# Attention and feed-forward on one core: key rows placed by DMA, first shift rows written by two engines, another order of the prologue and another schedule table

## The chip, the core and the metric

The kernel runs on one core of a Trainium2 chip. A core has a matrix engine (TensorE, PE in the profile, whose weight loads are listed as PEld), VectorE (DVE), ScalarE (ACT), GpSimd (POOL) and SyncE (SP, which here issues nearly all DMAs). Each engine runs its own instruction list in order; semaphores tie them together. The metric is the device time of one execution in microseconds; less is better.

## The reference

For a sequence of 2048 rows of width 512, the kernel mixes multi-query attention (32 heads of 16, one shared key and value head) with a feed-forward block, by a gate for each row:

```python
q = (x @ wq)                      # 32 heads of 16
k = x @ wk                        # one head, 16 wide
v = x @ wv
p = softmax(q @ k.T * 16 ** -0.5)
a = (p @ v) @ wo
b = silu(x @ w1) @ w2             # 512 -> 1792 -> 512
g = sigmoid((x * gate_w).sum(-1))
out = g * a + (1 - g) * b         # all in float32
```

## The kernel before

**Pairs of float16.** Each float32 operand of a product is split into a float16 upper part and a float16 rest; a product is the sum of three float16 matmuls (`product3`). For the scores the three terms are put into the contraction rows instead: per head group the moving tile `qb_[...]` holds, from partition 0 or 64 on, 16 rows of the queries' upper part, the same 16 again, 16 rows of their rest, and then two shift rows; `KT` holds against them the keys' upper part, their rest, their upper part, and two rows of the constant `ONE`. One matmul over 50 rows so gives the score less a shift that keeps the exponential in range.

**The prologue** (`first_pass`) loads x, transposes it on PE (`T00` to `T33`: chunk and tile), splits it on ScalarE and VectorE (`te`, `tl`), forms keys and values (`K0..`, `K1..`, four steps each over the contraction) and the first two blocks of queries (`Q0`, `Q1`). The order of all engines' work is written out by hand in the string `ORDER`; the name of each step stands for a function in the table `do`, and `BANK` gives the PSUM bank of each. Each engine's instructions run in the order in which these names appear. Before the change the steps behind the keys are:

- `k1`, `k2`: the keys' upper part (ScalarE) and rest (VectorE); `vr`: values and gate sums copied out of PSUM (ScalarE); `mx`, `mxa`, `prep`, `kab`: a bound on the keys by way of a maximum, a matmul and a mask;
- `pl0` to `pl3` (`k_places`): matmuls with 0/1 matrices `selA`, `selB` that put the keys of one chunk of 512 into their rows, and `KT0` to `KT3`, which copy them out of PSUM and add the constant rows (`m_one`); three on ScalarE, `KT3` on VectorE;
- `qs`, `ql`, `qa`: a query block's upper part, rest and absolute value; `qd` writes it to DRAM, and `lq` (`load_q`) reads it back into the rows of `qb_`, six DMAs for the first round;
- `bnd`, `s1`, `qbs`: the bound for each query (matmul with `kab`), its scaling to a shift row on ScalarE, and `shift_rows`, two DMAs that copy the first shifts into row 48 of each half of `qb_[0]`, with two more that store the shifts to DRAM (`q_shift`);
- `V`, `VO`, `sig`: transposed values and gate sums copied out by VectorE, and the gate's exponential on ScalarE; `lo`: range checks on VectorE; `st`, `sl`: first weight pieces; `d4`, `d2`: dummy matmuls.

**The attention loop** (`attention`) has 32 rounds (4 chunks of queries, 4 blocks, 2 halves) of 16 steps over the keys, and each step has two score groups: eight concurrent matmuls (line 1418) and one exponential over 128x1024 on ScalarE (line 1424), 1024 in all. Between score groups PE does the sums over the probabilities (line 1522), the feed-forward and projection products (line 1072), VectorE forms the low parts `L` of the probabilities (line 1443), and weight pieces come in one after another through two buffers `raw` (line 306 loads, 323 and 324 split). The order of all this is made when the program is built, by a small planner in the kernel: it keeps an estimated clock for each engine (`pe`, `act`, `dve`, `pool`) and chooses what PE and VectorE do next by twelve parameters (`Way`), which the table `WAYS` gives anew for every eight score groups. `SENT` is the planner's count of PE instructions sent at the loop's start and `BEHIND` VectorE's starting clock.

**The end.** The last four products are evicted by VectorE (line 1033) into `acc`, and SP sends each to the output (line 1036). Then every engine reads a flag and branches (lines 1671, 1672) past a second pass, which runs only if a range was left; SP passes the semaphores of the outstanding DMAs there. DMAs take eight semaphores in rotation.

Of the kernel before, what the change touches and what calls it, by code (L numbers as in the profile page):

```python
# [12 lines left out]
AF = mybir.ActivationFunctionType  # L13
OP = mybir.AluOpType
# [17 lines left out]
SENT, BEHIND = 162, 0.5  # L32
# [132 lines left out]
def kernel(  # L165
# [53 lines left out]
    kab = consts.tile([128, 32], F16)  # L219
# [142 lines left out]
    def masks(cst):  # L362
# [4 lines left out]
        hj = cst.tile([128, 32], F32)  # L367
        nc.gpsimd.iota(hj, pattern=[[16, 32]], base=0, channel_multiplier=0, allow_small_or_imprecise_dtypes=True)
# [11 lines left out]
        selA = cst.tile([128, 8, 16], F16)  # L380
        selB = cst.tile([128, 8, 16], F16)
        nc.gpsimd.memset(selA, 0.0)
        nc.gpsimd.memset(selB, 0.0)
        for b in (0, 2, 4, 6):
            nc.gpsimd.tensor_copy(selA[:, b], sel_k[:, b])
        for b in (1, 5):
            nc.gpsimd.tensor_copy(selB[:, b], sel_k[:, b])
# [14 lines left out]
    def load_q(q, c, o, rb, shifts):  # L402
# [3 lines left out]
        for f in range(2):  # L406
            b, queue = 64 * f, nc.sync
            queue.dma_start(q[b:b + 16], v[f, rb][:, :, 0])
            queue.dma_start(q[b + 16:b + 32], v[f, rb][:, :, 0])
            queue.dma_start(q[b + 32:b + 48], v[f, rb][:, :, 1])  # L410
            if shifts:
                queue.dma_start(q[b + 48:b + 48 + shifts], u[f, rb][0:shifts])
# [115 lines left out]
    def q_bound(pu, qa):  # L528

        for h in range(2):  # L530
            nc.tensor.matmul(pu[32 * h:32 * h + 32], kab[64 * h:64 * h + 64], qa[64 * h:64 * h + 64], start=True, stop=True)  # L531
# [6 lines left out]
    def first_pass():  # L538
        with ExitStack() as pro:
# [27 lines left out]
            rows = lambda c: slice(64 * (c % 2), 64 * (c % 2) + 16)  # L567
# [7 lines left out]
            BANK = {"T00": 7, "T01": 2, "T02": 4, "T03": 3, "T10": 7, "T11": 2, "Q0": 4, "T13": 3, "T20": 7, "T21": 2,  # L575
            "T23": 3, "T22": 5, "T12": 1, "T31": 7, "T30": 2, "T33": 3, "T32": 5, "K0": 1, "K1": 7, "Q1": 2, "pl1": 3,
            "pl0": 5, "prep": 4, "bnd": 1, "pl3": 3, "pl2": 7, "V0": 4, "V1": 5}
            BY_VECTOR = (3,)
            ORDER = """
            T00 T01 te00 te01 T02 tl00 T03 d4 tl01 te02 wkva tl02 te03 wkvd Wa0 tl03 Wd0 T10 T11 te10 Q00 te11 tl10  # L580
# [1120 lines left out]
```

## Time and profile before

| what | us |
|---|---|
| median of three runs (lowest, highest) | 1020.99 (1018.49, 1023.15) |
| the profiled execution | 1018.2 |
| its span, first to last instruction | 1016.3 |
| start of the span to the first exponential | 30.87 |
| first exponential to the end of the last | 968.7 |
| from there to the end of the span | 16.7 |
| ScalarE busy / PE busy / VectorE busy in the span | 988.3 / 1005.0 / 861.2 |

The times of the rows count from the first instruction of the span. A row of the timeline is: start, length, engine, line, operation, what it writes and reads with shapes, count of merged instructions, and in brackets how long the engine was idle before and what ended that. A row of a group ends in busy time, mean ns of one, and idle time before it. SPq is SP's queue issuing a DMA; the row doesn't show when it lands. The rows on which the argument rests are shown in the prediction.

### The profile page before, as it was taken

What the parts mean: (1) busy time and instruction counts of PE and PEld (TensorE: products, weight loads), DVE (VectorE), ACT (ScalarE), POOL (GpSimd) and SP (SyncE); (2) the same over time, 40 slices, a digit from 0 to 9 for tenths busy, and PEclk for the clock granted to TensorE, in tenths of its full rate; (3) what the DMA queues carried; (4) which work ended last, traced back from release to release, by engine and by line L of the source; (5) the groups of instructions that cost most, each with busy time, mean ns of one, the idle gap of its engine ahead of it and who ended that gap; (6) DMA issues with size and microseconds to landing.
All of it is one profiled execution on the core that took longest, in us unless ns stands there. A gap on an engine that the chain in (4) does not pass through costs nothing.

```text
span 1016.3 us, 67134 instructions
## 1 busy us (share of the span) xinstructions
PE 1005.0 (99%) x31724; PEld 586.7 (58%) x31724; DVE 861.2 (85%) x809; ACT 988.3 (97%) x1117; POOL 417.2 (41%) x278
## 2 busy tenths in 40 slices
PE   9999999999999999999999999999999999999997
PEld 5556656565555566656566566565556555555553
DVE  7888888898999998888888878888878878888886
ACT  6999999999999999999999999999999999999993
POOL 2053044362372245456345253835234264344620
PEclk9999999999999999999999999999999999999999
DMA  7212112000001100000001100000000100000001
GB/s 267 66 54 85 56 55 74 23 12 24 12 4 44 33 23 12 23 8 19 13 12 33 44 21 6 22 13 12 23 12 15 44 22 28 13 12 7 10 5 44
DMA packets 23314, 33.14 MB, mean 33 GB/s; under 512 B 5497, under 2 KB 14074, under 8 KB 23034
## 3 DMA queue, kind: packets, MB, share of 16 engines
q1 hardware_dynamic: 22602, 28.74, 8.8%
q8 instruction: 249, 4.08, 1.6%
q14 instruction: 31, 0.25, 0.1%
q10 hardware_dynamic: 432, 0.07, 0.0%
HBM read 20.26 MB, written 8.52 MB: 28 GB/s over the span
## 4 chain that ended last, share of the span: by engine, by line
PE 79%; ACT 15%; DVE 2%; issue 2%; DMA 1%; SPq 0%; DVEq 0%; ACTq 0%
PE pm L1072 30%; PE pv L1522 27%; PE S L1418 20%; ACT P L1424 14%; DVE L L1443 1%; ACT e L1086 1%; DMA xn<-in_A_x_dram 1%; PE b L595 1%; PE b L615 1%; PE pm L531 0%; DVE acc L1033 0%; PE b L247 0%; DVE mxs L257 0%; PE b L248 0%; PE b L249 0%
## 5 line engine op out<-in xcount | busy, mean ns | idle before, releaser
L1424 ACT ACTIVATE P<-S 128x1024 f32<-128x1024 f32 x1024 | 953.5, 1124 | 0.9 <-PE S L1418 0.5
L1443 DVE TENSOR_TENSOR L<-P 128x2048 f16<-128x2048 f32 x234 | 560.4, 2409 | 33.6 <-ACT P L1424 31.5
L1418 PE MATMUL S<-qb,KT 50*32 50x512 f16 x8192 | 439.8, 380 | 1.2 <-ACT P L1424 0.3
L1418 PEld LDWEIGHTS <-KT 50*32 50x32 f16 x8192 | 201.5, 89 | 240.5 <-issue 148.6
L1522 PE MATMUL pv<-P,VF 64*32 64x256 f32 (+1 forms) x6208 | 321.3, 468 | 0.0
L1072 PE MATMUL pm<-w2s,H 64*32 64x512 f16 x5184 | 264.9, 375 | 0.6 <-issue 0.5
L1072 PE MATMUL pm<-xs,w1s 64*32 64x512 f16 x5376 | 254.6, 375 | 0.0
L1093 POOL CAST H<-e 128x512 f16<-128x512 f32 x56 | 81.0, 1447 | 247.6 <-DVE e L1091 247.6
L1344 POOL TENSOR_TENSOR U<-T,U 128x512 f32<-128x512 f32 x31 | 83.2, 2682 | 229.0 <-DVE U L1339 229.0
L1522 PEld LDWEIGHTS pv<-P,VF 64*32 64x32 f32 x6208 | 126.7, 106 | 32.5 <-issue 3.2
L1072 PEld LDWEIGHTS <-H 64*32 64x32 f16 x5184 | 117.8, 92 | 37.4 <-issue 1.6
L1072 PEld LDWEIGHTS <-w1s 64*32 64x32 f16 x5376 | 110.6, 92 | 42.9 <-issue 1.8
L1094 POOL TENSOR_TENSOR H<-e,H 128x512 f16<-128x512 f32 x56 | 107.6, 1922 | 4.5
L1522 PE MATMUL pv<-P,VP 64*32 64x512 bf16 x1872 | 103.6, 387 | 0.0
L1072 PE MATMUL pm<-xs,wqs 64*32 64x512 f16 x1344 | 100.7, 375 | 0.0
L1522 PE MATMUL pv<-L,VP 64*32 64x512 f16 x1872 | 100.4, 374 | 0.0
L1522 PEld LDWEIGHTS <-VP 64*32 64x32 f16 x3744 | 65.4, 92 | 29.0 <-issue 6.7
L1091 DVE SCALAR_TENSOR_TENSOR e<-e,pm 128x512 f32<-128x512 f32 x56 | 38.4, 686 | 41.5 <-ACT e L1086 41.0
L1072 PE MATMUL pm<-wo_s,O 64*32 64x512 f16 x1440 | 66.5, 375 | 0.0
L1372 POOL CAST O<-T 128x512 f16<-128x512 f32 x15 | 23.3, 1556 | 73.5 <-DVE T L1370 73.5
L1345 POOL TENSOR_TENSOR C<-U 128x240 f32<-128x240 f32 x31 | 51.3, 1656 | 2.4
L1033 DVE SCALAR_TENSOR_TENSOR acc<-pm,g,acc 128x512 f32<-128x512 f32 x46 | 34.2, 746 | 19.3 <-PE pm L1072 19.2
(174 smaller groups left out, 535.6 us busy)
## 6 DMA issues: line engine op xcount, KB each, us to landing
qb<-qd SPq DMA_DIRECT2D x192, 32.0 KB
raw<-in_B_w_dram SPq DMA_DIRECT2D x22, 256.0 KB
xn<-in_A_x_dram SPq DMA_DIRECT2D x8, 512.0 KB
out_dram<-acc SPq DMA_DIRECT2D x16, 256.0 KB
qd<-qx SPq DMA_DIRECT2D x14, 256.0 KB
w1r<-in_B_w_dram SPq DMA_DIRECT2D x2, 512.0 KB
raw<-in_A_wo_dram SPq DMA_DIRECT2D x4, 256.0 KB
qb<-sh SPq DMA_DIRECT2D x62, 2.0 KB
```

The source lines that it names most:

```text
L1033: nc.vector.scalar_tensor_tensor(a, po, gate[:, n:n + 1], a, op0=OP.mult, op1=OP.add)
L1072: nc.tensor.matmul(self.bank[32 * m:32 * m + 32], l(i, rows, 32 * m), r(j, rows), start=first, stop=last)
L1091: nc.vector.scalar_tensor_tensor(e, e, 1.0, ph, op0=OP.add, op1=OP.mult)
L1093: nc.gpsimd.tensor_copy(H[:, 0], e)
L1094: nc.gpsimd.tensor_tensor(H[:, 1], e, H[:, 0], op=OP.subtract)
L1344: eng.tensor_tensor(U, T, U, op=OP.add)
L1345: eng.tensor_tensor(C[:, :, 1:16], z[:, :, 1:16], z[:, :, 17:32], op=OP.add)
L1372: eng.tensor_copy(O[:, 0], OT)
L1418: nc.tensor.matmul(sc[32 * m:32 * m + 32, f], KT[b:b + 50, k0:k0 + 32], qtile[i][b:b + 50, j], start=True, stop=True)
L1424: nc.scalar.activation(P[:, 2 * j:2 * j + 2], sc, AF.Exp, scale=scale_of(c, o))
L1443: nc.vector.tensor_tensor(L[s], P, upper(P), op=OP.subtract)
L1522: nc.tensor.matmul(pvs[i][h][32 * j:32 * j + 32, cols], a[r], b[r, j, cols], start=start, stop=rest == n)
```

## The change

The layout of the contraction rows changes: the two shift rows now stand at 32 and 33 of each half (and the constant rows of `KT` with them), and the third group of 16 at 34 to 49.

- The keys are put into `KT` by DMA from `k1` and `k2` (`ka`, `kb`: 24 DMAs on SP in all) and no more by `pl` and `KT`; the constant rows are written at the start by four VectorE instructions. `selA` and `selB` aren't made in the first pass.
- The first shifts are computed by four small matmuls (`bq0`, `bq1`), whose result stands in partitions 32 and 96, and written straight into `qb_[0]` by ScalarE (`sq0`) and VectorE (`sq1`), two instructions each over one partition. `bnd` and `s1` remain for the stored shifts (`qsh`).
- The second query block is stored by two DMAs instead of one.
- `BANK` and `ORDER` are written anew; `WAYS` has another 128 entries; `SENT` is 158 for 162, `BEHIND` 1.0 for 0.5.
- At the very end a memset of one column of the output tile `accs[13]`, the second of the last four, and a one-column matmul on it are added. The count of DMAs ahead of the last output changes, and with it the semaphore that it takes.
- The second pass (not run here) follows the new layout.

```diff
-SENT, BEHIND = 162, 0.5
+SENT, BEHIND = 158, 1.0
 WAYS = [
...
-            queue.dma_start(q[b + 32:b + 48], v[f, rb][:, :, 1])
+            queue.dma_start(q[b + 34:b + 50], v[f, rb][:, :, 1])
             if shifts:
-                queue.dma_start(q[b + 48:b + 48 + shifts], u[f, rb][0:shifts])
+                queue.dma_start(q[b + 32:b + 32 + shifts], u[f, rb][0:shifts])
...
+            for c in range(NCH):
+                nc.vector.tensor_scalar(KT[:, c * 512:c * 512 + 512], still, m_one, None, op0=OP.add)
             constants()
...
             ORDER = """
-            T00 T01 te00 te01 T02 tl00 T03 d4 tl01 te02 wkva tl02 te03 wkvd Wa0 tl03 Wd0 T10 T11 te10 Q00 te11 tl10
-            T13 tl11 Q01 te13 T20 tl13 T21 te20 T23 te21 tl20 T22 te23 T12 tl21 te22 T31 tl23 te12 T30 tl22 te31 Q02
-            te30 tl12 T33 tl31 T32 te33 tl30 K000 te32 tl33 Q03 st0 tl32 st1 K010 sl0 Wa1 qs0 K100 st3 ql0 K020 qa0
-            sl3 qd0 K110 st2 sl1 K030 sl2 K120 k10 Wd1 lq vr0 K130 k20 mx0 Q10 k11 pl1 vr1 mx1 Q11 KT1 mxa pl0 k21
-            prep Q12 KT0 kab bnd lo Q13 s1 pl3 qs1 qbs pl2 KT3 V0 qa1 ql1 V1 d2 KT2 VO0 VO1 qd1 sig
+            T00 T01 te00 te01 T03 tl00 wkva T02 d4 tl01 Wa0 te02 wkvd Wd0 te03 T11 tl02 T10 te11 tl03 te10 T13
+            tl11 Q00 te13 tl10 T12 tl13 T20 te12 Q01 te20 tl12 T22 tl20 T21 te22 T23 te21 tl22 T30 te23 T31
+            tl21 te30 Q02 tl23 te31 T32 tl30 Wa1 Q03 tl31 te32 T33 tl32 qs0 K000 te33 ql0 K010 qa0 Wd1 qd0 st3
+            K020 tl33 st0 K030 sl3 st2 K100 sl0 vr0 lq K110 k10 sl2 st1 K120 mx0 K130 k20 sl1 Q10 k11 ka00
+            kb00 Q11 vr1 mx1 mxa Q12 ka01 kb01 prep kab k21 Q13 qs1 bq0 bq1 sq0 sq1 ka10 ka11 V0 V1 qa1 ql1
+            bnd d4 s1 lo kb10 kb11 VO0 VO1 qsh qd1 sig
             """
...
+            def into_KT(r, k, a, h):
+                for b in (r, 64 + r):
+                    nc.sync.dma_start(KT[b:b + 16, 512 * (2 * a + h):512 * (2 * a + h) + 512], k[64 * h:64 * h + 16])
...
+            to_shift = dict(scale=-2.0 ** 10 / ONE, bias=SHIFT * LAM / ONE)
+            def first_bound(p):
+                for f in range(2):
+                    r = slice(64 * f + 32, 64 * f + 64)
+                    nc.tensor.matmul(on(f"bq{p}")[r], kab[64 * p:64 * p + 64, 2 * f:2 * f + 32], qa[0][64 * p:64 * p + 64], start=True, stop=True)
+            def first_shift(p):
+                for f in range(2):
+                    r = slice(64 * f + 32, 64 * f + 33)
+                    if p:
+                        nc.vector.tensor_scalar(qb_[0][r, p], on(f"bq{p}")[r], to_shift["scale"], to_shift["bias"], op0=OP.mult, op1=OP.add)
+                    else:
+                        nc.scalar.activation(qb_[0][r, p], on(f"bq{p}")[r], AF.Copy, **to_shift)
...
+                for h in range(2):
+                    do[f"ka{a}{h}"] = lambda a=a, h=h: (into_KT(0, k1[a], a, h), into_KT(34, k1[a], a, h))
+                    do[f"kb{a}{h}"] = lambda a=a, h=h: into_KT(16, k2[a], a, h)
...
                 add_out(NCH - 1, t, banks[t], g1)
+            sent_ = accs[NKT - 3][:, 0:1]
+            nc.vector.memset(sent_, 0.0)
+            nc.tensor.matmul(banks[0][0:1, 0:1], sent_, sent_, start=True, stop=True)
             return
```

More of the change, by code (lines that the diff above doesn't have):

```diff
@@ L218 @@
     wqs = consts.tile([128, 2, KD, D], F16)
-    kab = consts.tile([128, 32], F16)
+    kab = consts.tile([128, 64], F16)
     qx = consts.tile([128, 1024], F16)
@@ L277, in __init__ @@
             self.s1, self.s2, self.so, self.sq = s1, s2, so, sq
-            self.todo, self.raws, self.rest, self.done, self.count, self.queue = list(range(len(pieces))), [], [], [], 0, nc.gpsimd
+            self.todo, self.raws, self.rest, self.done, self.count, self.queue = list(range(len(pieces))), [], [], [], 0, nc.sync
             self.end, self.clock = {}, lambda: 0.0
@@ L379, in masks @@
         nc.vector.tensor_scalar(flat(sel_k), flat(mj), pm, None, op0=OP.is_equal)
[L380 to L387, printed above, removed]
+        selA = selB = None
+        if places:
+            selA = cst.tile([128, 8, 16], F16)
+            selB = cst.tile([128, 8, 16], F16)
+            nc.gpsimd.memset(selA, 0.0)
+            nc.gpsimd.memset(selB, 0.0)
+            for b in (0, 34, 64, 98):
+                nc.gpsimd.tensor_copy(flat(selA)[:, b:b + 16], sel_k[:, 0])
+            for b in (16, 80):
+                nc.gpsimd.tensor_copy(flat(selB)[:, b:b + 16], sel_k[:, 0])
         rm = cst.tile([128, 2], F32)
-        nc.vector.tensor_scalar(rm[:, 0:1], pm, 48.0, None, op0=OP.is_lt)
-        nc.vector.tensor_scalar(rm[:, 1:2], pm, 50.0, None, op0=OP.is_lt)
+        nc.vector.tensor_scalar(rm[:, 0:1], pm, 32.0, None, op0=OP.is_lt)
+        nc.vector.tensor_scalar(rm[:, 1:2], pm, 34.0, None, op0=OP.is_lt)
         m_one = cst.tile([128, 1], F32)
@@ L394, in masks @@
         nc.vector.tensor_scalar(hj, hj, pm, None, op0=OP.subtract)
-        hm = cst.tile([128, 2, 32], F32)
+        hm = cst.tile([128, 2, 64], F32)
         nc.vector.tensor_scalar(hm[:, 0], hj, 0.0, None, op0=OP.is_le)
         nc.vector.tensor_scalar(hm[:, 1], hj, -15.0, None, op0=OP.is_ge)
-        hmask = cst.tile([128, 32], F32)
+        hmask = cst.tile([128, 64], F32)
         nc.vector.tensor_tensor(hmask, hm[:, 0], hm[:, 1], op=OP.mult)
@@ L530, in q_bound @@
         for h in range(2):
-            nc.tensor.matmul(pu[32 * h:32 * h + 32], kab[64 * h:64 * h + 64], qa[64 * h:64 * h + 64], start=True, stop=True)
+            nc.tensor.matmul(pu[32 * h:32 * h + 32], kab[64 * h:64 * h + 64, 0:32], qa[64 * h:64 * h + 64], start=True, stop=True)
     def q_shift(o, c, s1):
@@ L553, in first_pass @@
                 nc.tensor.matmul(still_at, still[:, 0:128], still, start=True, stop=True)
-            sel_k, selA, selB, m_one, hmask = masks(sb)
+            sel_k, _, _, m_one, hmask = masks(sb, False)
             xn, wqr, wkv, first = loads(sb, 256, True)
+            for c in range(NCH):
+                nc.vector.tensor_scalar(KT[:, c * 512:c * 512 + 512], still, m_one, None, op0=OP.add)
             constants()
@@ L573, in first_pass @@
             at, do = {}, {}
[L575 to L578, printed above, removed]
+            BANK = {"T00": 7, "T01": 3, "T03": 5, "T02": 4, "T11": 7, "T10": 3, "T13": 4, "Q0": 5, "T12": 7, "T20": 3,
+                    "T22": 4, "T21": 7, "T23": 2, "T30": 3, "T31": 1, "T32": 4, "T33": 7, "K0": 2, "K1": 3, "Q1": 7,
+                    "prep": 1, "V0": 5, "bnd": 2, "bq1": 1, "bq0": 0, "V1": 4}
             ORDER = """
-            T00 T01 te00 te01 T02 tl00 T03 d4 tl01 te02 wkva tl02 te03 wkvd Wa0 tl03 Wd0 T10 T11 te10 Q00 te11 tl10
-            T13 tl11 Q01 te13 T20 tl13 T21 te20 T23 te21 tl20 T22 te23 T12 tl21 te22 T31 tl23 te12 T30 tl22 te31 Q02
-            te30 tl12 T33 tl31 T32 te33 tl30 K000 te32 tl33 Q03 st0 tl32 st1 K010 sl0 Wa1 qs0 K100 st3 ql0 K020 qa0
-            sl3 qd0 K110 st2 sl1 K030 sl2 K120 k10 Wd1 lq vr0 K130 k20 mx0 Q10 k11 pl1 vr1 mx1 Q11 KT1 mxa pl0 k21
-            prep Q12 KT0 kab bnd lo Q13 s1 pl3 qs1 qbs pl2 KT3 V0 qa1 ql1 V1 d2 KT2 VO0 VO1 qd1 sig
+            T00 T01 te00 te01 T03 tl00 wkva T02 d4 tl01 Wa0 te02 wkvd Wd0 te03 T11 tl02 T10 te11 tl03 te10 T13
[4 more added lines that the diff above has]
+            bnd d4 s1 lo kb10 kb11 VO0 VO1 qsh qd1 sig
             """
@@ L648, in ranges @@
                     absmax(mxs[:, m:m + 1], wkvs[:, 0, :, a:a + n], AX.XY)
-            def shift_rows():
-                for p in range(2):
-                    nc.sync.dma_start(qb_[0][48:113:64, p], s1[32 * p:32 * p + 3:2])
-                q_shift(0, 0, s1)
+            to_shift = dict(scale=-2.0 ** 10 / ONE, bias=SHIFT * LAM / ONE)
[10 more added lines that the diff above has]
+                        nc.scalar.activation(qb_[0][r, p], on(f"bq{p}")[r], AF.Copy, **to_shift)
             for c in range(NCH):
@@ L672, in first_pass @@
                 do[f"qa{a}"] = lambda a=a: nc.scalar.activation(qa[a], qs_[a][:, 0], AF.Abs)
-                do[f"qd{a}"] = lambda a=a: nc.sync.dma_start(qd[a, 0], qs_[a])
+                do[f"qd{a}"] = lambda a=a: [nc.sync.dma_start(qd[a, 0][r], qs_[a][r]) for r in ((slice(0, 128),), (slice(0, 64), slice(64, 128)))[a]]
                 do[f"k1{a}"] = lambda a=a: nc.scalar.activation(k1[a][both], on(f"K{a}")[both], AF.Copy, scale=k_to)
@@ L679, in first_pass @@
                 do[f"VO{a}"] = lambda a=a: V_out(a)
-            for c in range(NCH):
-                do[f"pl{c}"] = lambda c=c: k_places(on(f"pl{c}"), k1[c // 2], k2[c // 2], selA, selB, rows(c))
-                do[f"KT{c}"] = lambda c=c: KT_out(c, c in BY_VECTOR)
+                for h in range(2):
+                    do[f"ka{a}{h}"] = lambda a=a, h=h: (into_KT(0, k1[a], a, h), into_KT(34, k1[a], a, h))
+                    do[f"kb{a}{h}"] = lambda a=a, h=h: into_KT(16, k2[a], a, h)
+            for p in range(2):
+                do[f"bq{p}"] = lambda p=p: first_bound(p)
+                do[f"sq{p}"] = lambda p=p: first_shift(p)
             def still_busy(n):
@@ L692, in first_pass @@
             do["bnd"] = lambda: q_bound(on("bnd"), qa[0])
-            do["s1"] = lambda: nc.scalar.activation(s1, on("bnd")[0:64], AF.Copy, scale=-2.0 ** 10 / ONE, bias=SHIFT * LAM / ONE)
-            do["qbs"] = shift_rows
+            do["s1"] = lambda: nc.scalar.activation(s1, on("bnd")[0:64], AF.Copy, **to_shift)
+            do["qsh"] = lambda: q_shift(0, 0, s1)
             do["lq"] = lambda: load_q(qb_[0], 0, 0, 0, 0)
@@ L918, in row_maxima @@
                 for rb in range(2):
-                    qt = load_q(gs.tile([128, 2, 512], F16, name="qs", bufs=1), c, o, rb, 0)
+                    qt = gs.tile([128, 2, 512], F16, name="qs", bufs=1)
+                    for b in (32, 96):
+                        nc.vector.memset(qt[b:b + 2], 0.0)
+                    load_q(qt, c, o, rb, 0)
                     for p in range(2):
@@ L927, in row_maxima @@
                                     pm_ = gp.tile([128, 512], F32, name="pt")
-                                    nc.tensor.matmul(pm_, qt[b:b + 48, p, t * 128:t * 128 + 128],
-                                                     KT[b:b + 48, k * 512:k * 512 + 512], start=True, stop=True)
+                                    nc.tensor.matmul(pm_, qt[b:b + 50, p, t * 128:t * 128 + 128],
+                                                     KT[b:b + 50, k * 512:k * 512 + 512], start=True, stop=True)
                                     nc.vector.tensor_reduce(mb[:, k:k + 1], pm_, axis=AX.X, op=OP.max)
```

60 lines of the change are left out of this document (25 added, 35 removed), and 113 rows, old and new, of the table WAYS.

## The prediction

> **What bounds the kernel now.** I read the span by stages first, then the group of the exponentials, then ScalarE's order of time, and last the prologue's order of time on each engine.
>
> ```profile
> 10.00:30.00 20.00, 20.00 (x138) 11.53 (x137) 16.91 (x37) 15.90 (x29) 1.24 (x12) 1.00 0.56 205
> 30.90:999.60 968.70, 966.90 (x31474) 566.47 (x31466) 829.82 (x736) 967.84 (x1080) 410.82 (x235) 1.00 0.09 26
> ```
>
> ```profile
> L1424 ACT ACTIVATE P<-S 128x1024 f32<-128x1024 f32 x1024 | 953.5, 1124 | 0.9 <-PE S L1418 0.5
> ```
>
> ```profile
> 819.14 0.73 ACT L1086 ACTIVATE e<-pm 128x512 f32<-128x512 f32 x1
> 819.62 5.76 ACT L1424 ACTIVATE P<-S 128x1024 f32<-128x1024 f32 x6
> 825.04 0.83 ACT L1086 ACTIVATE e<-pm 128x512 f32<-128x512 f32 x1
> ```
>
> The columns of the stages are window, length, then busy time of PE, PEld, DVE, ACT, POOL, clock, DMA share, GB/s. The attention loop is 968.7 of the 1016.3 us, and ScalarE is busy in 967.84 of them: its 1024 exponentials and 56 tanh run end to end, so the loop can only shorten where they follow each other more tightly. The tightest they go stands in the last three rows: six exponentials take 825.04 - 819.62 = 5.42 us, 0.903 each, and a tanh 819.62 - 819.14 = 0.48. So the loop's floor is 1024 x 0.903 + 56 x 0.48 = 951.6 us; 17.1 us of lateness lie in the loop, and that is all that the new table has to play with. From 10 to 30 us PE is busy all the time: in the prologue matmul work counts one for one until another engine is later. Which one is, the end of the prologue shows:
>
> ```profile
> 13.38 5.47 DVE L606 SCALAR_TENSOR_TENSOR xs<-b,xs 128x512 f16<-128x512 f32 x9 [0.42 <-ACT xs L604]
> 18.80 4.72 PE L615 MATMUL b<-xs,wkvs 128*64 128x512 f16 x42
> 20.06 0.69 DVE L606 SCALAR_TENSOR_TENSOR qs__248<-b,qs__248 128x512 f16<-128x512 f32 x1 [0.61 <-ACT qs__248 L604]
> 23.57 0.59 ACT L674 ACTIVATE k<-b 80x512 f16<-80x512 f32 x1 [0.22 <-PE b L615]
> 23.99 1.26 DVE L257 TENSOR_REDUCE mx<-k 80x1 f32<-80x512 f16 x2
> 25.36 0.30 DVE L637 TENSOR_REDUCE mxa<-mx 16x1 f32<-16x2 f32 x2
> 26.03 0.38 PE L689 MATMUL b<-mxa,sel_k 80*128 80x2 f32 x2
> 26.64 0.24 DVE L641 TENSOR_SCALAR kab<-hmask,kv__242 128x32 f16<-128x32 f32 x1
> 26.80 0.15 DVE L644 TENSOR_SCALAR lo<-kv__242 128x1 f32<-128x1 f32 x1
> 27.01 0.39 PE L531 MATMUL b<-qa,kab 64*32 64x512 f16 x2
> 27.11 0.41 DVE L257 TENSOR_REDUCE mxs<-wkvs 128x1 f32<-128x64 f16 x3
> 27.33 0.39 PE L247 MATMUL b<-xs,wqs 128*128 128x512 f16 x1
> 27.44 0.59 ACT L693 ACTIVATE s<-b 64x512 f16<-64x512 f32 x1 [0.62 <-PE b L531]
> 28.05 1.23 SPq L652 DMA_DIRECT2D qb<-s  x2
> 28.09 0.39 PE L479 MATMUL b<-k,selA 16*128 16x512 f16 x2
> 28.62 1.09 PE L626 MATMUL b<-ident,vr 128*128 128x128 f32 x8
> 28.72 0.75 DVE L620 TENSOR_SCALAR KT<-b,m_one 128x512 f16<-128x512 f32 x1 [1.21 <-PE b L480]
> 29.39 0.68 DVE L606 SCALAR_TENSOR_TENSOR qs__249<-b,qs__249 128x512 f16<-128x512 f32 x1
> 30.07 0.11 PEld L1418 LDWEIGHTS <-KT 50*32 50x32 f16 x8 [0.42 <-DMA qb<-s]
> 30.46 0.16 DVE L632 COPY gg<-b 128x8 f32<-128x8 f32 x1
> 30.65 0.22 ACT L484 ACTIVATE gg<-gg 128x16 f32<-128x16 f32 x1 [0.62 <-DVE gg L632]
> ```
>
> Two chains end here within half a microsecond. The scores start at 30.08, when the first shifts (bnd, s1, qbs) have come back by DMA: 28.05 to 30.07 is 2.02 us. But the first exponential stands behind sig (L484) on ScalarE, and sig waits 0.62 us for VectorE's last copy, VO1, which ends at 30.62. So both have to come earlier.
>
> **The change part by part.** *Shift rows.* The DMA of 2.02 us goes; sq0 (two ACTIVATEs on ScalarE) and sq1 (two TENSOR_SCALARs on VectorE) take its place. One partition of 512 numbers isn't in the trace; the nearest rows read PSUM over 64 partitions, L693 above with 0.59 and this one:
>
> ```profile
> L1304 DVE TENSOR_SCALAR e<-pm 64x512 f16<-64x512 f32 x14 | 9.5, 680 | 10.1 <-PE pm L531 9.9
> ```
>
> ```profile
> 7.01 2.10 DVE L606 SCALAR_TENSOR_TENSOR xs<-b,xs 128x512 f16<-128x512 f32 x3 [3.78 <-ACT xs L604]
> 20.78 0.33 SPq L673 DMA_DIRECT2D qd<-qs__248  x1
> 22.84 0.32 SPq L408 DMA_DIRECT2D qb<-qd  x1
> 25.07 0.42 SPq L410 DMA_DIRECT2D qb<-qd  x1
> ```
>
> Two such in a row take 1.26 us (L257 at 23.99), the second starting 0.6 behind the first, so I cost sq1 and sq0 at 1.2 us each; the bounds are 0.3 (two instructions like L632's 0.16) and 1.4.
>
> *PE.* The pl matmuls go: 28.09 to 28.62 for the last two pairs, so 0.53 a pair-step and three of them, 1.6 us. bq0 and bq1 come: four matmuls like L531's two, which hold PE from 27.01 to 27.33, so 0.64. d2 becomes d4, two dummies more at 0.22 each. Net 1.6 - 0.64 - 0.44 = 0.5 us less, and the scores could start at about 29.5. The new order of T, Q and K moves work only inside the stretch in which PE is full, so the last K product ends where it did (18.80 + 4.72 = 23.5), give or take the one Q step that moves across it. A K step of six matmuls in pairs, like a Q step of three, is 0.65 us (seven in 4.72, the last one's tail included). Wa1, now ahead of te32, delays the last transposes on ScalarE by one such instruction, 0.6; K100, which needs them, has four K steps, 2.6 us, ahead of it.
>
> *Keys by DMA.* 24 DMAs of 16 partitions on SP. In the rows above six DMAs of the query rows start 0.45 us apart (22.84 to 25.07 is five steps), and qd takes 2.06 from its issue until the first that waits for it is issued. qd0 follows ql0 (20.06 now), which moves ahead of the last tl, of Wd1 and the w1 pieces: the nine tl of the first row end at 18.85, 0.6 apart, so ql0 starts in the place of the last, some 18.5 with Wa1 ahead of it. So qd is issued at 19.2, lq from 21.3 to 24.0, ka00 and kb00 from 24.0 to 26.7, and the last of chunk 0 lands 2.06 us after its issue at 26.3: 28.4. That is ahead of the scores by one microsecond, so I cost it at nothing; if that cover is gone (lq as late as it is now, 25.5), it lands at 29.9 and the scores are 0.4 late. By a rule of the Trainium skill (DMA: Bandwidth & Descriptors, section Rules for kernel authors: many small transfers are to be coalesced, those under 64 KB are mostly overhead) 24 transfers of 16 KB are the wrong form; by its fixed 2.0 us paid one after another, the six of chunk 0 would take 12 us. The rows speak against a price paid serially: six DMAs of 32 KB leave SP in 2.7 us while the first is still on its way. The other 18 and qsh, qd1 (2 each) are queued behind. Chunk 1 is first read at the ninth exponential, 7 us into the loop, and lands by 31. The constant rows of KT, four VectorE writes at the start, lie in the 3.78 us for which VectorE waits ahead of 7.01: 4 x 0.75 (as KT3) would still fit; if not, tl00 is late by what is over.
>
> *VectorE, the one that decides.* KT3 (28.72 to 29.39, 0.67) goes; sq1 (1.2) comes. lo now runs while VectorE waits for pl3 (26.80 to 27.52 with 1.21 idle behind it); in the new order it stands between ql1 and VO0, and k21 behind kab: both lose their cover. Step by step from the same k11 at 23.57: mx1 no longer stands behind k20 and mx0 and follows k11's end (24.16) at once, 24.8, mxa 0.4 later; prep is then held by Q10 to Q12 (23.46 + 3 x 0.65 = 25.4) and not by two pl's, 0.6 earlier than 26.03; kab ends at 26.88 - 0.63 = 26.25. Then k21 0.61, a wait of 0.2 for bq1 (Q13 to 26.35, bq0 and bq1 to 27.05), sq1 1.2, ql1 0.60, lo 0.72, VO0 and VO1 0.62: 30.2. sig takes 0.04 + 0.22, the first exponential starts at **30.5 instead of 30.87: -0.4 us**. ScalarE (sq0, qa1, s1 by 29.1) and PE (scores at 29.5) are both done before. So of a DMA of 2 us that goes, 0.4 is gained, because what is late next is VectorE's gg.
>
> *The end.*
>
> ```profile
> 1008.18 2.96 SPq L1036 DMA_DIRECT2D out_dram<-acc  x4
> L1672 SPq EVENT_SEMAPHORE  x8: 17/17/17, 1014.1 to 1014.6; - x8
> ```
>
> SP passes eight semaphores in a fixed order, all of them between 1014.1 and 1014.6, 3 us behind the last issue: the first is the one of the last output, and the other seven, long done, follow in 0.5 us. The semaphores rotate over the DMAs; 24 + 1 - 2 = 23 more is one place back, from first to eighth. Then seven are passed while the last output is on its way: **-0.5 us**. The memset and matmul of sent_ wait for the second of the four outputs, issued some 2 us ahead of the last; PE and VectorE have nothing behind them but their branch, and SP passes the last semaphore after that. Nothing; if it did land last, 0.5 would be lost.
>
> *Table, SENT, BEHIND.* SENT goes down by 4, two instructions for each of two matmuls fewer (eight pl's and two bq pairs with two dummies: 8 - 4 - 2). The 128 entries decide at which exponential each matmul group and each VectorE task is put; the amount of work doesn't change. No row prices it: the bounds are -17.1 (no lateness at all) and, by the same size, as much again. I take 0, since nothing in the trace tells a sign.
>
> **Sum.** -0.4 - 0.5 + 0 = -0.9 us. The profiled execution took 1018.2 us (span 1016.3 and 1.9 around it), so it would be 1017.3; the three runs shown have a median of 1020.99, 2.8 above it. On that median: **1020.1 us**.
>
> **The rivals.** (1) *The table takes lateness away.* For it: the loop has 17.1 us that no exponential needs. Against it: the lateness is spread, not in one place that a table could mend. A third of it is 5.7 us: 1014.4.
>
> (2) *The queue on SP makes the kernel slower.* Behind the 24 key DMAs stand qsh, qd1 and the eight DMAs of the next round's queries; the first reload of raw is behind all.
>
> ```profile
> 35.65 0.35 SPq L306 DMA_DIRECT2D raw<-in_B_w_dram  x1
> 41.02 0.42 DVE L323 TENSOR_SCALAR w1s<-raw 128x512 f16<-128x512 f32 x1
> 42.50 0.69 DVE L1091 SCALAR_TENSOR_TENSOR e<-e,pm 128x512 f32<-128x512 f32 x1 [0.33 <-ACT e L1086]
> 44.34 2.92 DVE L1443 TENSOR_TENSOR L<-P 128x2048 f16<-128x2048 f32 x1 [1.15 <-ACT P L1424]
> ```
>
> 24 + 2 + 2 + 8 DMAs at 0.45 from 24.0 end at 40.2; the reload, issued at 35.65 now and used at 41.02, would land between 42.3 (2.06 as qd) and 45.6 (5.4 as now until used). VectorE then stands still at the third piece, with the tanh's gate and the first L behind it, and PE's sums behind those. It decides from a landing later than 41.0; 1.5 us of idle time (0.33 and 1.15) absorb the near end. I price it at 2 us, 1022.1, slower than before by 1.1. For it: the reload surely is some 4.5 us later. Against it: VectorE's idle time, and the exponentials run ahead of the sums by several steps.
>
> (3) *The table adds lateness*, a third more: 1025.8. (4) *sig is not the bound*, because sq1 or lo is cheaper; then the scores decide: start at 29.5 and the exponential 0.45 behind, 29.95, that is -0.9 and with the end 1019.6. (5) *The change doesn't do what it says*: the last output isn't on the eighth semaphore, 1020.6.
>
> **How the numbers follow.** Forecast 0.50, rival (1) 0.18, (2) 0.12, (3) 0.07, (4) 0.10, (5) 0.03. The range takes in the forecast with the spread of the three runs (1018.5 to 1023.2), (2), (4), (5) and most of (1), and leaves (3) out: 1014 to 1024.5. 0.5% is 5.1 us, about what a measurement of this kernel can tell from no change. Below 1015.9: most of (1) and a little of the forecast, 0.17. Above 1026.1: half of (3), the far end of (2), 0.06. Between: 0.77.
>
> **What would show it.** First exponential at 30.5 with sig still waiting for VO1 in front of it; PE idle or in dummies ahead of it; the L1672 waits of SP with seven passed before the last landing; SP's first raw load at about 40 us. Wrong would be: a first exponential before 30.0 (VectorE isn't the bound), one after 31 (the keys' DMAs are), VectorE waiting for raw near 41 us, or a loop whose 968.7 us moved by more than 3 us: then the table did it.

## The result and the profile after

| | before | after |
|---|---|---|
| median of six runs each (lowest, highest), us | 1022.33 (1018.49, 1023.15) | 1031.47 (1030.17, 1033.42) |
| the profiled execution / its span | 1018.2 / 1016.3 | 1031.64 / 1029.8 |
| start of the span to the first exponential | 30.87 | 30.23 |
| first exponential to the end of the last | 968.7 | 985.4 |
| from there to the end of the span | 16.7 | 14.2 |

The changed kernel is slower: ratio 1.0094, 95% interval 1.0081 to 1.0108. Start and end became shorter, as forecast and more; the loop between them became 16.7 us longer.

The start, in the order of time after the change (columns as before):

```profile
26.74 1.39 DVE L667 TENSOR_SCALAR qb<-b 1x512 f16<-1x512 f32 x2
26.95 1.19 ACT L669 ACTIVATE qb<-b 1x512 f16<-1x512 f32 x2
29.66 0.62 PE L1440 MATMUL S<-qb,KT 50*32 50x512 f16 x15 [0.31 <-DMA KT<-k]
30.06 0.21 ACT L491 ACTIVATE gg<-gg 128x16 f32<-128x16 f32 x1 [0.65 <-DVE gg L638]
30.23 1.02 ACT L1446 ACTIVATE P<-S 128x1024 f32<-128x1024 f32 x1
```

sq1 (L667) and sq0 (L669) take 1.39 and 1.19 us; sig (L491) again waits for VectorE's last copy of gg, 0.65 us, and the first exponential (L1446, before L1424) stands right behind it, 0.64 us earlier than before.

The loss begins in SP's queue. Four groups of its order of time:

```profile
24.39 16.27 SPq L628 DMA_DIRECT2D KT<-k  x24
40.76 0.77 SPq L543 DMA_DIRECT2D sh<-s  x2
41.63 1.46 SPq L689 DMA_DIRECT2D qd<-qs__243  x2
47.50 0.36 SPq L311 DMA_DIRECT2D raw<-in_B_w_dram  x1
```

The 24 key DMAs occupy SP for 16.27 us, 0.68 each with two pauses of about half a microsecond in it. raw is issued at 47.50 instead of 35.65. What waits for it shows in the waits from 30 to 80 us (releaser; then us in total, times, longest):

```profile
DVE w1s L328 <- DMA raw<-in_B_w_dram: 10.7, 1, 10.7
ACT P L1446 <- PE S L1440: 9.9, 3, 8.7
PE pm L1094 <- DVE e L1113: 8.0, 1, 8.0
```

and, link by link, in the order of time:

```profile
50.37 0.43 DVE L328 TENSOR_SCALAR w1s<-raw 128x512 f16<-128x512 f32 x1 [10.68 <-DMA raw<-in_B_w_dram]
51.44 0.68 DVE L1113 SCALAR_TENSOR_TENSOR e<-e,pm 128x512 f32<-128x512 f32 x1
52.17 1.48 PE L1094 MATMUL pm<-xs,w1s 64*32 64x512 f16 x24 [7.95 <-DVE e L1113]
54.20 1.02 ACT L1446 ACTIVATE P<-S 128x1024 f32<-128x1024 f32 x1 [8.72 <-PE S L1440]
55.85 1.02 ACT L1446 ACTIVATE P<-S 128x1024 f32<-128x1024 f32 x1 [0.62 <-PE S L1440]
57.40 1.02 ACT L1446 ACTIVATE P<-S 128x1024 f32<-128x1024 f32 x1 [0.53 <-PE S L1440]
```

VectorE's list is in order, so the gate of the tanh (L1113) stands behind the split of raw (L328), PE's next product behind the gate, and the scores behind that product: ScalarE stands still for 8.72 us. The two exponentials behind wait for PE again, and the windows say why (window, length, busy PE, PEld, DVE, ACT, POOL, clock, DMA share, GB/s):

```profile
44.00:46.00 2.00, 0.22 (x8) 0.00 (x0) 0.00 (x0) 1.49 (x2) 0.00 (x0) 1.00 0.37 85
48.00:50.00 2.00, 0.00 (x0) 0.00 (x0) 0.00 (x0) 0.00 (x0) 0.00 (x0) 0.50 0.52 136
54.00:56.00 2.00, 2.00 (x53) 0.84 (x42) 1.97 (x3) 1.18 (x2) 1.92 (x2) 0.50 0.00 0
58.00:60.00 2.00, 2.00 (x72) 1.00 (x64) 1.06 (x2) 2.00 (x4) 0.30 (x1) 1.00 0.31 103
```

While PE idles its granted clock falls to half, and it is still at half when PE works again: 24 matmuls take 1.48 us, where 24 of the same form take 0.84 us at the full clock (run 12 below). So the stall costs 9.9 us in all, by the row of the waits. The Trainium skill (TensorE: Matmul & The Clock Gate, section Part 1: The HAM clock gate) gives an idle window of some 3.4 us for the fall to half and about as long a busy time for the way back. This trace agrees only in the size of the step: by its clock records the clock is at half from 46.66 to 56.90, 10.24 us or three times 3.41, but the fall comes 2.4 us after PE's last matmul (44.22) and the way back 4.7 us after PE is at work again (52.17).

The end:

```profile
1024.17 2.31 SPq L1058 DMA_DIRECT2D out_dram<-acc  x4
1027.04 0.06 DVE L1671 MEMSET acc<- 128x1 f32 x1 [0.92 <-DMA out_dram<-acc]
L1697 SPq EVENT_SEMAPHORE  x8: 17/17/17, 1027.1 to 1028.4; - x8
```

The last output is now the eighth that SP passes, at 1028.4, and the span ends 1.4 us later; before, the first pass came 2.2 us ahead of the end. The four outputs leave SP in 2.31 us instead of 2.96, and the last is passed 1.9 us after its issue is over (1024.17 + 2.31 = 1026.48) instead of 3.0 (1011.14 to 1014.1).

The two spans differ by 13.5 us: start -0.64, stall +9.9, end -2.5, and +6.7 spread over the rest of the loop. Of these 6.7, 4.1 can be put down to the execution and not to the change: the profiled one of before lies that far below the median of its six runs, the one of after at its median. That all of the 4.1 lies in the loop is assumed. 2.6 us are left to explain.

### The profile page after: what moved, and what is told of

The parts are those of the page before. It is cut to its first block, busy times and chain, and to the rows that moved or that the text cites. A ratio compares the mean times of both kernels' runs of the same rounds, so it can differ in the third digit from the quotient of the medians.

```text
span 1029.8 us, 67810 instructions
## 1 busy us (share of the span) xinstructions
PE 1010.4 (98%) x32044; PEld 599.9 (58%) x32044; DVE 858.8 (83%) x814; ACT 990.2 (96%) x1116; POOL 407.3 (40%) x270
## 4 chain that ended last, share of the span: by engine, by line
PE 68%; ACT 22%; DVE 4%; issue 3%; SPq 1%; DMA 1%; ACTq 0%; DVEq 0%
PE pm L1094 26%; PE pv L1544 23%; ACT P L1446 21%; PE S L1440 17%; DVE L L1465 1%; PE b L603 1%; ACT e L1108 1%; PE b L623 1%; DMA xn<-in_A_x_dram 0%; DVE acc L1055 0%; DMA raw<-in_B_w_dram 0%; SPq L628 0%; DMA out_dram<-acc 0%; DVE e L1113 0%; PE b L252 0%
## 5 line engine op out<-in xcount | busy, mean ns | idle before, releaser
L1446 ACT ACTIVATE P<-S 128x1024 f32<-128x1024 f32 x1024 | 955.0, 1109 | 14.8 <-PE S L1440 13.3
L1465 DVE TENSOR_TENSOR L<-P 128x2048 f16<-128x2048 f32 x233 | 554.8, 2395 | 33.1 <-ACT P L1446 31.7
L1440 PE MATMUL S<-qb,KT 50*32 50x512 f16 x8192 | 457.0, 381 | 1.6 <-DMA KT<-k 0.3
L1544 PE MATMUL pv<-P,VF 64*32 64x256 f32 (+1 forms) x6544 | 330.7, 453 | 0.2 <-issue 0.2
L1094 PE MATMUL pm<-xs,w1s 64*32 64x512 f16 x5376 | 263.3, 378 | 9.1 <-DVE e L1113 8.6
L1544 PEld LDWEIGHTS pv<-P,VF 64*32 64x32 f32 x6544 | 136.3, 106 | 37.6 <-issue 3.7
L1094 PEld LDWEIGHTS <-w1s 64*32 64x32 f16 x5376 | 116.9, 93 | 55.3 <-issue 16.2
L1544 PE MATMUL pv<-L,VP 64*32 64x512 f16 x1864 | 105.5, 375 | 0.2 <-issue 0.2
L1116 POOL TENSOR_TENSOR H<-e,H 128x512 f16<-128x512 f32 x56 | 99.8, 1782 | 4.5
L1113 DVE SCALAR_TENSOR_TENSOR e<-e,pm 128x512 f32<-128x512 f32 x56 | 38.4, 685 | 41.3 <-ACT e L1108 41.1
L1394 POOL CAST O<-T 128x512 f16<-128x512 f32 x15 | 29.3, 1955 | 72.7 <-DVE T L1392 72.7
L1094 PEld LDWEIGHTS <-wqs 64*32 64x32 f16 x1344 | 42.7, 92 | 12.7 <-issue 1.4
```

The source lines that it names most:

```text
L1094: nc.tensor.matmul(self.bank[32 * m:32 * m + 32], l(i, rows, 32 * m), r(j, rows), start=first, stop=last)
L1113: nc.vector.scalar_tensor_tensor(e, e, 1.0, ph, op0=OP.add, op1=OP.mult)
L1116: nc.gpsimd.tensor_tensor(H[:, 1], e, H[:, 0], op=OP.subtract)
L1394: eng.tensor_copy(O[:, 0], OT)
L1440: nc.tensor.matmul(sc[32 * m:32 * m + 32, f], KT[b:b + 50, k0:k0 + 32], qtile[i][b:b + 50, j], start=True, stop=True)
L1446: nc.scalar.activation(P[:, 2 * j:2 * j + 2], sc, AF.Exp, scale=scale_of(c, o))
```

## The experiments

Two theories. **Q**: the key DMAs hold SP's queue, raw is late, and with it VectorE, PE and ScalarE. **T**: the table, which sets the order in the loop, is worse. Ratios are to the kernel before, on the same chip, with 95% intervals.

**1. Keys on another queue.** Only the six key DMAs of the first chunk stay on SP.

```diff
-nc.sync.dma_start(KT[b:b + 16, ...], k[64 * h:64 * h + 16])
+queue = nc.gpsimd if a or h else nc.sync
+queue.dma_start(KT[b:b + 16, ...], k[64 * h:64 * h + 16])
```

> The changed kernel with 18 of the 24 key DMAs (all but those of chunk 0) issued from GpSimd and not from SP. Theory Q (the queue on SP: the first reload of raw stands behind the key DMAs, VectorE waits 10.7 us for it, PE 8 and ScalarE 8.7 behind it): SP issues raw at about 36 us as in the kernel before, VectorE's wait for raw is below 1 us, and some 10 us go: 1031.5 - 10 = 1021.5, with the lateness of 6.5 us spread over the rest of the loop still there. Theory T (the new table puts VectorE's and PE's tasks wrongly, and raw is only what they happen to wait for): a wait of the same size under another name, 1030 or more.

```profile
24.27 3.81 SPq L629 DMA_DIRECT2D KT<-k  x6
35.84 0.36 SPq L311 DMA_DIRECT2D raw<-in_B_w_dram  x1
```

1022.96 us, 1.0015 (0.9995 to 1.0035). raw is issued where it was before the change, no wait for it is left, and the loss is gone but for what can't be told from none.

**2. The changed kernel with the old table.** `WAYS`, `SENT` and `BEHIND` of before; all else stays.

> The changed kernel with the table, SENT and BEHIND of the kernel before. Theory Q: VectorE still waits some 9 to 11 us for raw; only the spread lateness of 6.5 us may go: 1025 if the table made it, 1031 if it follows from the wait. Theory T: no long wait, 1020 to 1022.

```profile
DVE w1s L323 <- DMA raw<-in_B_w_dram: 9.4, 1, 9.4
```

1030.37 us, 1.0073 (1.0053 to 1.0093). The stall is there with either table, and most of the loss with it. In this trace the clock is at half for another 3.41 us near the start of the loop, from 31.43 on, as this window shows (columns as above):

```profile
32.00:34.00 2.00, 2.00 (x38) 1.78 (x34) 1.75 (x11) 1.55 (x2) 0.00 (x0) 0.50 0.14 34
```

In the 3.41 us ahead of it PE had no idle time over 0.95 us.

**3. The kernel before with the new table.** The same edit the other way round.

> The kernel before with the new table, SENT 158 and BEHIND 1.0. Theory Q: no wait for raw over 1 us; the spread lateness alone, 1022.3 + 6.5 = 1029 if the table makes it, 1022 if it doesn't. Theory T: the whole loss, 1032 or more.

1025.59 us, 1.0027 (1.0014 to 1.0040), with no wait for raw. So T holds as well, for 2.8 us (1.4 to 4.1): the size of the 2.6 that were left.

**4. The kernel before with 24 DMAs added on SP.** They come at the end of the prologue and copy 16 partitions by 1 KB of the split input to a scratch tensor that nobody reads.

```diff
+for n in range(24):
+    nc.sync.dma_start(extra[n], xs[0:16, 0, 0, 0:512])
```

> The kernel before with 24 more DMAs of 16 partitions by 1 KB from SP ahead of the loop, into a scratch that nothing reads. Theory Q: they take SP 0.5 to 0.64 us each, 12 to 15 us, raw is issued at 47 to 50 instead of 35.65, VectorE waits 8 to 12 us for it, and the time is 1030 to 1034. Theory T: the queue costs nothing, 1022 to 1024.

```profile
30.12 14.46 SPq L703 DMA_DIRECT2D extra<-xs  x24
48.70 0.36 SPq L307 DMA_DIRECT2D raw<-in_B_w_dram  x1
ACT P L1427 <- PE S L1421: 11.0, 2, 10.4
```

1033.57 us, 1.0111 (1.0094 to 1.0127). Without any new key path, shift row or table the whole loss comes back, as the same chain: ScalarE waits 10.4 us.

**5. raw on another queue.** All key DMAs stay on SP, the weight pieces are loaded from GpSimd.

```diff
-split_pieces.queue = nc.sync
+split_pieces.queue = nc.gpsimd
```

> The changed kernel with nothing but the queue of the weight-piece loads changed: raw is issued from GpSimd, and all 24 key DMAs stay on SP. Theory Q (raw is late only because it stands behind the key DMAs in SP's queue): raw is issued by 36 us or earlier, VectorE's wait of 10.7 us for it is gone, PE doesn't stand still near 44 to 52 us and its clock stays at 1.00; time as with the keys on GpSimd, ratio 1.000 to 1.004 (1022 to 1026). Rival (the key DMAs load the DMA engines, so that any transfer beside them is late): raw lands at 45 us or later though it is issued early, VectorE waits 4 us or more, ratio 1.006 or more.

```profile
24.06 17.89 SPq L628 DMA_DIRECT2D KT<-k  x24
32.35 0.71 POOL L311 DMA_DIRECT2D raw<-in_B_w_dram  x1 [21.95 <-DVE T L512]
39.10 0.42 DVE L328 TENSOR_SCALAR w1s<-raw 128x512 f16<-128x512 f32 x1
40.00:60.00 20.00, 19.58 (x632) 10.93 (x631) 14.33 (x12) 19.27 (x23) 11.31 (x9) 1.00 0.23 59
```

1020.62 us, 0.9999 (0.9987 to 1.0011). The key DMAs take SP even longer, 17.89 us, and it costs nothing: raw is there before VectorE asks for it, and the clock stays at 1.00. What counted was the place in SP's queue, not the load on the DMA engines.

**6. Both mended.** The edits of 1 and 2 together.

> The changed kernel with the 18 key DMAs not of the first chunk issued from GpSimd and with the table, SENT and BEHIND of before. If queue and table add up (keys on GpSimd alone 1.0015, the new table alone on the kernel before 1.0027): 1.0015 - 0.0027 = 0.9988, about 1021.3, the start 0.3 to 0.6 us earlier and the end 2 us shorter than before as what is gained. Rival (the table is tuned for the new prologue, so that the old one costs here what it saves there): ratio 1.0015 to 1.004.

1018.32 us, 0.9969 (0.9957 to 0.9982): the one version of the changed prologue that is faster than the kernel before, though not clearly by more than the two effects add up to (0.9988, itself known to some 0.002). In its trace the first exponential is at 31.06 and the end takes 14.6 us, so the gain shows at the end and not at the start. Against the same kernel with the new table (1.0015) the old one is worth 0.46% here.

**7. Fewer DMAs.** As 4, with 7 of them.

> The kernel before with 7 small DMAs of 16 partitions added on SP at the end of the prologue, where the run with 24 of them gave 1.0111. Threshold theory (what counts is whether raw lands before the first product needs it and PE stands still long enough to lose its clock): raw is issued at 39 to 40 us, VectorE waits for it 0 to 2 us, PE's clock stays at 1.00, ratio 0.999 to 1.002. Rival (each DMA costs its share wherever it stands): 7/24 of 1.1%, ratio 1.003 to 1.004. In both the last output takes the eighth semaphore, as after the change: if that alone shortens the end, from the last exponential to the end of the span it is 14.5 to 16.2 instead of 16.7; if not, 16.5 to 18.

```profile
40.28 0.36 SPq L307 DMA_DIRECT2D raw<-in_B_w_dram  x1
DVE w1s L324 <- DMA raw<-in_B_w_dram: 2.7, 1, 2.7
ACT P L1427 <- PE S L1421: 1.5, 1, 1.5
```

1021.40 us, 0.9999 (0.9987 to 1.0011). VectorE waits longer than the expected 2 us, ScalarE 1.5, and the time doesn't show it. By chance raw is issued here at 40.28, where the prediction put it for the changed kernel: one DMA of the query rows holds SP for 1.71 us, where its neighbours take 0.42 to 0.56, and this execution is the longest of the ten (1025.3).

```profile
37.87 1.71 SPq L411 DMA_DIRECT2D qb<-qd  x1
1015.26 4.04 SPq L1039 DMA_DIRECT2D out_dram<-acc  x4
```

The end, 16.8 us with the last output passed as the eighth, isn't shorter, but the gain is only hidden: the four outputs take SP 4.04 us instead of 2.96, and from the end of their issue to the end of the span it is 4.1 us instead of 5.2.

**8. The end without its two new instructions.** The memset and the one-column matmul on `sent_` are taken out of the changed kernel.

> The changed kernel without the memset and the one-column matmul at the very end; all else stays. Theory S (these two hold back PE's and VectorE's branch, whose instruction fetch otherwise stands in the way of the output DMAs): the second of the last four outputs is held for about 1.3 us again, the last lands 3.5 to 4 us behind its eviction instead of 2.3, the end from the last exponential is 15.2 to 16 us instead of 14.2, ratio to the kernel before 1.010 to 1.011. Rival (the end is shorter by the semaphore's place alone, the hold is chance): end 14.0 to 14.6, ratio 1.009 as the changed kernel.

```profile
1023.65 2.31 SPq L1058 DMA_DIRECT2D out_dram<-acc  x4
L1694 SPq EVENT_SEMAPHORE  x8: 17/17/17, 1026.5 to 1030.0; - x8
L1694 PEldq COMPARE_BRANCH  x1: 2254/2254/2254, 1023.1 to 1023.1; - x1
```

and in the changed kernel, for PE's branch:

```profile
L1697 PEldq COMPARE_BRANCH  x1: 509/509/509, 1028.0 to 1028.0; - x1
```

1033.12 us, 1.0109 (1.0090 to 1.0128), which can't be told from the changed kernel; the trace can. Theory S expected an output to be held at its issue; none is. But the last is passed at 1030.0, 4.0 us behind the end of its issue (1025.96) instead of 1.9, and the end takes 16.3 us instead of 14.2. PE's branch now runs while the outputs are on their way and takes 2.25 us instead of 0.51. So the two instructions are worth 2.1 us between these two traces, and the place of the hold was wrong. All fourteen traces say the same: the seven with the two instructions have an end of 14.2 to 15.0 us, the seven without (before, runs 3, 4, 7, 8, 11, 12) 16.3 to 18.0.

**9. raw on GpSimd with the old table.** The edits of 5 and 2 together.

> The changed kernel with the weight pieces loaded from GpSimd and with the table, SENT and BEHIND of before; all key DMAs stay on SP. The same kernel with the new table gave 0.9999. If the new table costs in every surrounding (0.0027 on the kernel before; with the keys on GpSimd 1.0015 against 0.9969, that is 0.0046): 0.995 to 0.9975. Rival (the table costs only where the keys are on GpSimd): 0.9985 to 1.001.

1021.04 us, 1.0000 (0.9987 to 1.0012): the rival. Here the tables are alike, so the price of a table isn't a constant that can be carried from one surrounding to another.

**10. The two instructions alone**, added to the kernel before.

```diff
+sent_ = accs[NKT - 3][:, 0:1]
+nc.vector.memset(sent_, 0.0)
+nc.tensor.matmul(banks[0][0:1, 0:1], sent_, sent_, start=True, stop=True)
```

> The kernel before with nothing but the two instructions at the very end added (the memset on a column of the second of the last four output tiles and the one-column matmul on it), so that PE and VectorE read the flag only after the second output has landed. Theory S, as the run without them showed (the end 16.3 instead of 14.2, the last output landing 4.3 us behind its issue instead of 2.25): the last output lands 2.2 to 2.4 us behind its issue, SP issues the four outputs without the hold of 1.3 us, the end from the last exponential is 14.7 to 15.2 instead of 16.7, ratio 0.997 to 0.9995. Rival (the two instructions take effect only with the eighth semaphore, or not at all): end 16 to 17, ratio 0.9995 to 1.001.

```profile
1010.34 2.31 SPq L1036 DMA_DIRECT2D out_dram<-acc  x4
L1675 SPq EVENT_SEMAPHORE  x8: 17/17/17, 1014.5 to 1015.1; - x8
```

1018.68 us, 0.9986 (0.9975 to 0.9997). The end is 15.0 us instead of 16.7, with the last output still the first that SP passes, at 1014.5, 1.9 us behind its issue. That is 1.7 us for the two instructions; from 15.0 to the 14.2 of the changed kernel is what the eighth place adds, 0.8: from the last output's pass to the end of the span it is 2.2 us here and 1.4 there.

**11. 24 DMAs of another form.** As 4, each of 128 partitions by 128 bytes.

```diff
+    nc.sync.dma_start(extra[n], xs[:, 0, 0, 0:64])
```

> The kernel before with 24 DMAs added on SP as in the run that gave 1.0111, each again of 16 KB, but of 128 partitions by 128 bytes in place of 16 partitions by 1 KB. If the form sets the time that SP spends (qd of 128 partitions takes 0.33 us, the DMAs of 16 partitions 0.60): the 24 take 8 to 9.5 us, raw is issued at 43 to 45 us, ScalarE stands still 4.4 to 6.5 us there (by the runs with 7 and with 24: 1.5 us at an issue at 40.3, 10.4 at 48.7, about 1.06 us for each us of lateness), ratio 1.004 to 1.007. Rival (SP's time goes by the number of DMAs, or by descriptors): 14 us or more, raw at 48.5 or later, ScalarE still for 10 us or more, ratio 1.010 or more.

```profile
30.08 15.33 SPq L703 DMA_DIRECT2D extra<-xs  x24
49.54 0.36 SPq L307 DMA_DIRECT2D raw<-in_B_w_dram  x1
```

1032.87 us, 1.0119 (1.0094 to 1.0143). The form with many partitions isn't cheaper: 0.64 us each. What makes qd cheap at 0.33 stays open.

**12. Between 7 and 24.** As 4, with 12.

> The kernel before with 12 of the DMAs of 16 partitions added on SP: between the runs with 7 (0.9999) and with 24 (1.0111). SP spends 7 to 8 us on them, raw is issued at 42.5 to 44 us, ScalarE stands still 3.8 to 5.5 us there. Theory (the time goes by when raw is issued, from a point at about 39 us on, 1 us for 1 us): ratio 1.003 to 1.006. Within it: PE is idle for 4 us or more, and if idling is what halves its clock, the windows after it show less than 1.00 for some us, with exponentials late beyond the stall by 0.5 to 1.5 us in total; with 7 DMAs the idle 1.7 us left the clock at 1.00. Rival (a fixed price as soon as PE stands still): ratio 1.009 or more.

```profile
41.41 0.36 SPq L307 DMA_DIRECT2D raw<-in_B_w_dram  x1
ACT P L1427 <- PE S L1421: 2.9, 1, 2.9
46.71 0.84 PE L1075 MATMUL pm<-xs,w1s 64*32 64x512 f16 x24 [3.17 <-DVE e L1094]
46.00:48.00 2.00, 1.29 (x48) 0.79 (x55) 2.00 (x3) 0.17 (x1) 1.28 (x1) 1.00 0.34 108
```

1025.65 us, 1.0054 (1.0033 to 1.0075). SP was faster than expected (0.55 us each), so raw went out at 41.41 and ScalarE waited 2.9 us. PE idle for 3.17 us kept its clock here: the same 24 matmuls take 0.84 us. But the profiled execution is the shortest of the four, 1021.84 us with a mean granted clock of 0.999; the other three take 1025.21 to 1026.57 with 0.996 to 0.997. That fits a clock that fell in those three: by an estimate, 3.41 us at half lower the mean over the span by 0.0017, so 0.002 to 0.003 would be one or two such stretches. They are 3.4 to 4.7 us longer, but that isn't the price of the fall alone, as the kernel before scatters over 3.7 us in the same batch (1018.90 to 1022.58); and their traces aren't there to show it.

The runs in the order of raw's issue:

| run | raw issued at | ScalarE stands still | PE idle | clock after | ratio |
|---|---|---|---|---|---|
| before | 35.65 | - | - | 1.00 | 1 |
| 7 DMAs | 40.28 | 1.5 | 1.7 | 1.00 | 0.9999 |
| 12 DMAs (profiled execution) | 41.41 | 2.9 | 3.2 | 1.00 | 1.0054 (all four) |
| run 8 | 47.05 | 8.6 | 7.8 | 0.50 | 1.0109 |
| the change | 47.50 | 8.7 | 8.0 | 0.50 | 1.0094 |
| 24 DMAs | 48.70 | 10.4 | 9.8 | 0.50 | 1.0111 |
| run 2 | 48.81 | 9.0 | 8.4 | 0.50 | 1.0073 |
| 24, other form | 49.54 | 11.4 | 10.8 | 0.50 | 1.0119 |

From first to last run with a stall, ScalarE stands still 9.9 us longer for 9.3 us of lateness: from an issue at about 39 us on, every microsecond counts about once in ScalarE's wait, and where PE's clock falls the slow clock comes on top. The length of the idle time alone doesn't decide whether it falls: the clock fell 2.4 us after PE's last matmul in the changed kernel, 5.3 us after it in run 8 (43.80 to 49.08), not at all within 3.17 us in run 12, while near the start of the loop in run 2 it fell behind idle times of 0.95 and 0.31. It stood at half for 3.41, 6.83, 10.24 or 13.65 us (runs 2, 8, the change, 11), in each a multiple of 3.41.

## Why the prediction was wrong

**The start: right.** Forecast -0.4, measured -0.64, by the mechanism that was named: VectorE's gg decides, and the 2 us of the DMA are not gained in full. sq1 was costed at 1.2 and took 1.39. That the size came out so near is in part luck: the seven traces with the old prologue have the first exponential at 30.36 to 30.87, the seven with the new one at 29.79 to 31.06, and the middle values, 30.56 and 30.23, lie 0.33 apart. The keys of the first chunk just came in time: of all the scores only one group waited for them, 0.31 us, and nothing behind it was late. The cover of 1 us that the prediction counted on was gone, though. In runs 2 and 6, with the key DMAs starting 0.5 and 0.8 us later (24.87, 25.20), PE stood still for 0.95 and 1.24 us ahead of the first scores, and the first exponential then waited 0.8 us for them behind sig; that it was the keys is likely and not shown.

**The queue on SP: at nothing in the sum, the right mechanism as rival (2), at the wrong size.** The failed term is the 0.45 us for each of "24 + 2 + 2 + 8 DMAs", taken from the query loads. The key DMAs took 0.68, which makes 5.5 of the 7.3 us between the forecast issue at 40.2 and the real one at 47.50; the other twelve took 0.57 each (40.66 to 47.50), 1.4; the queue began 0.4 later. The bound had to come from the slowest row of SP: the DMA pair in the prologue rows of before, 1.23 us for qb<-s, is 0.62 each, and 36 of those from 24.0 on end at 46.1. At the issue that was forecast the wait was about right: run 7 had raw issued at 40.28 and ScalarE waiting 1.5 us, against the 2 us in the prediction, though its time (0.9999) shows no loss. Seven microseconds later the same mechanism costs 9.9.

**"A few steps ahead" was no cover.** The prediction held that idle time of VectorE and the exponentials' lead over the sums would absorb a late raw. They absorb an issue of raw up to about 39 us, and nothing after. PE holds scores and feed-forward products in one list, so a missing weight piece stops the scores as well. And the fall of PE's clock behind such a stall was not in the sum at all: at least 1.15 us here (0.62 and 0.53).

**The table: 0 was too low, within the bounds.** 2.8 us (1.4 to 4.1) on the kernel before, 0.46% with the keys on GpSimd, nothing with raw on GpSimd. Which of its entries cost it wasn't tried, nor why it matters in one surrounding and not in another.

**The end: right in what was forecast, short of the rest.** The eighth place was put at -0.5; it is 0.8 between run 10 and the changed kernel, 0.4 between the kernel before and run 8, and hidden by a longer issue of the outputs in run 7. The two instructions were put at "Nothing" and gave -1.7 to -2.1 (runs 10 and 8). That the outputs are through sooner when PE's and VectorE's branches wait is shown by runs 8 and 10; which of the two branches is in the way, and by what resource (the fetch of instructions or the read of the flag), wasn't tried.

**The sum.** Forecast -0.9 on the median of 1020.99; measured +9.1 between the medians of six. By its terms: start -0.64, stall +9.9, table +2.8 (its price on the kernel before, which need not hold here), end -2.5, that is +9.6.

## What to carry to other kernels

An engine that issues DMAs is a queue like any other: when DMAs are put into it, take the time of each from the slowest rows of that queue, add them up, and look for the next load behind them that somebody waits for, however far behind it stands. A load that feeds an in-order engine has a date from which on every microsecond is lost in full; find that date in the trace of before (last idle time ahead of the first use) and keep small transfers on another queue if they push it past. Here it was enough to move either of the two, the small transfers or the load.

## What the runs showed of the hardware

- SP spent 0.55 to 0.75 us on each of a row of small DMAs from SBUF (7 to 24 of 16 KB, runs 4, 5, 7, 11, 12 and the change), whether 16 partitions by 1 KB or 128 by 128 bytes. GpSimd took 0.49 each for the 18 keys of run 1 (8.77 us). The Trainium skill (DMA: Bandwidth & Descriptors, section Issuing engines are not separate DMA queues) says that issuing from several engines saves only the time to initiate, "which is usually small relative to the DMA itself"; here one initiating, 0.68 us, is short too beside the 1.8 us (median) from issue to landing of the keys that GpSimd issued in run 1, but 24 in a row held SP for 16.27 us and made the load behind them late, and that was the loss.
- Now and then one DMA holds SP for 0.5 to 1.3 us more than its like: two of the 24 key DMAs took 1.07 and 1.14 us instead of 0.59, in the kernel before the second of the last four outputs 1.34 instead of 0.36, and in run 7 a query load 1.71 instead of 0.42. What sets these pauses wasn't tried.
- The clock's fall may be a dear part of a short stall: in run 12, where ScalarE's wait was 2.9 us, the executions with a lower mean clock were longer by 3.4 to 4.7 us. How much of that is the clock isn't shown.
- PE's granted clock fell to half with PE idle for 2.4 us only (the change, 44.22 to 46.66) and stayed at 1.00 through 3.17 us (run 12), and it stood at half for multiples of 3.41 us (3.41 in run 2, 6.83 in run 8, 10.24 in the change, 13.65 in run 11).
